# More buffers for the first 256 queries' attention, row blocks of layer 1 one step apart, one operand distance

## The chip, the cores and the metric

The kernel runs on one core of a Trainium2 chip. The metric is the device time of one execution in microseconds (us). The engines are TensorE (PE, matrix products; PEld is its loading of the stationary operand), VectorE (DVE), ScalarE (ACT), GpSimd (POOL) and SyncE (SP, which issues the DMAs here). SBUF is the on-chip memory, PSUM holds the results of products.

## The reference

Block-causal attention, 4 batches of 8 heads with 576 positions of 64, then two expert layers on the 2304 tokens. The weights are float64.

```
scores = q @ k^T / sqrt(64), masked where block_i < block_j (blocks of 64)
attn   = softmax(scores) @ v                      # 4 x 8 x 576 x 64
x      = attn as 2304 x 512
h      = x @ w_in                                 # 512 -> 2048
g      = max(h, 0) + log1p(exp(-|h|))             # softplus
x2     = g @ w_out                                # 2048 -> 512
h2     = x2 @ u_in                                # 512 -> 1024
solu   = h2 * softmax(h2)
out    = (layer_norm(solu) * g_ln) @ u_out        # 1024 -> 512
```

## The kernel before

**Number format.** Products run in fp32r. Each float32 matrix is split into a high and a low part, and a product is the sum of three (high·high, high·low, low·high). The float64 weights come as two 32-bit words and are unpacked by a `Piece` (L255): `load` (L267) on SP into one of 3 `raw` buffers, `abs` on ACT (L274), three bit steps on DVE (L277, L280, L284), the high part by a copy on ACT or DVE, and the low part by a subtraction on DVE (L294). There are 32 pieces for layer 1, 16 w1 and 16 w2.

**Attention of the first 256 queries.** `UnitA` (from L479), 16 units, unit n for batch n // 4 and a pair of heads. A unit loads qkA (256 KB) and vA (128 KB) on SP, makes scores on PE (`mm_qk`, into a PSUM bank R, r, acc or hp), masks them with a memset and takes maxima on DVE (L538, L543, L546), exponentiates on ACT into eA (L552), normalizes on DVE (four `norm` instructions, L564), transposes on PE (L571), copies the result to SBUF (`psA`), multiplies by v (`pv`), and splits the result into xt (`x_hi`, `x_lo`, L590), the input of layer 1. Buffers: qkA 3, vA 2, the small mA and dA 2 each, eA 2, psA 1. The remaining 320 queries of a batch (`UnitC`) come after all 16 units and all weights, in other banks.

**Layer 1** is made of pairs (`Pair`): pair (c, p) takes columns of row block c (256 tokens) and two of the 16 slices of the 2048 features. Block a (24 products `hp<-xt,w`, 12 for each slice) gives h; softplus follows (ACT abs, exp, ln; DVE t at L656; gh; DVE gl at L664); block b (24 products with gh, gl and w2) adds into the accumulator of the row block: acc for c = 0, R for c = 1. SEQ is the order of the pairs: for row blocks 0 and 1 it runs LAG steps ahead in row block 0; LAG is 2, so (0,0), (0,1), (1,0), (0,2), (1,1) and so on. Row blocks 2 to 8 run one after the other. **Layer 2** (`Tok`) runs on 18 tiles of 128 tokens.

**The order of everything** is computed by `Plan` (L43): a list scheduler that gives each step to its engine's queue by rank and by modelled durations. The tables OFF and RANK shift the ranks of a kind of step or of a group; MARGIN adds to the modelled latencies. The order on each engine is fixed when the program is built; the engines wait for one another by semaphores.

**Placement.** A product of 256 columns reads a stationary and a moving tile from SBUF. By the addresses of the built program, the start of the moving operand minus that of the stationary one, modulo 512 bytes, is 192 for 1512 of these 3456 products (1296 with xt and w1, 216 with gh or gl and the last w2 tiles) and 448 for the other 1944. Small tiles set it: `pad_x`, `pad_l` and the 64 extra elements in `wide`.

Of the kernel before, what the change touches and what calls it, by code (L numbers as in the profile page):

```python
# [10 lines left out]
F32 = mybir.dt.float32  # L11
F32R = mybir.dt.float32r
# [6 lines left out]


OFF = {
    "Pair.a": -160.87, "Pair.b": -32.19, "Pair.do_gh": -103.91, "Piece.bits0": 139.36, "Piece.do_lo@P": -201.40,
    "Piece.do_lo_g": 267.76, "Tok.a": 141.06, "Tok.x_hi": -460.68, "UnitA.x_hi": 408.37, "Tok.tr": -394.45,
    "Tok.bm": 359.77, "UnitC.pv": 348.22, "UnitC.tr": -288.31, "Pair.stt": -191.35, "Pair.do_gl": -445.21,
    "UnitC.qk_lo": -290.12,
}
RANK = {
# [3 lines left out]
    "Tok": (4285.47, -27.327),  # L31
}
MARGIN = {
    "PE": 600.0, "ACT": 100.0, "DVE": 100.0, "POOL": 100.0,
# [2 lines left out]
B, H, S, D = 4, 8, 576, 64  # L37
# [15 lines left out]
class Plan:  # L53
# [8 lines left out]
    def add(self, eng, dur, rank, fn, deps=(), lat=None):  # L62
        t = _Task()
        t.key = key_of(fn)

        t.alts = dict(eng) if isinstance(eng, dict) else {eng: dur}
        name, i = t.group = self.group
        t.local = rank
        t.rank = rank + RANK[name][0] + RANK[name][1] * i + OFF.get(t.key, 0.0) + OFF.get(t.key + "@" + name, 0.0)
        t.eng, t.fn, t.n, t.done = None if len(t.alts) > 1 else eng, fn, len(self.tasks), False  # L70
        t.lat = (self.LAT + (120.0 if eng == "PE" else 0.0)) if lat is None else lat
        t.users, t.left, t.ready = [], 0, 0.0
        for d in deps:
            if d is not None:
                d.users.append(t)
                t.left += 1
        self.tasks.append(t)
        return t
# [5 lines left out]
    def chain(self, eng, rank, steps, deps):  # L84
        for dur, fn in steps:
            t = self.add(dur if isinstance(dur, dict) else eng, dur, rank, fn, deps)
            deps = [t]
        return t
# [83 lines left out]
def key_of(fn):  # L172
    while isinstance(fn, partial):
        fn = fn.func
    return ".".join(fn.__qualname__.split(".")[-2:])
# [6 lines left out]
def dve_ns(n, per=1.04):  # L182
    return 70.0 + per * n
# [6 lines left out]
def dma_ns(nbytes, n=1):  # L190
    return max(50.0 + nbytes / 360.0, 550.0 * n)
# [3 lines left out]
def body(ctx: ExitStack, tc: tile.TileContext, qk, qkA, vP, vA, w1, w2, u1, u2, gln, out):  # L195
    nc = tc.nc
    PE, ACT, DVE, POOL, SP = nc.tensor, nc.scalar, nc.vector, nc.gpsimd, nc.sync
    plan = Plan()
    XTB, LAG = 3, 2
    add, chain = plan.add, plan.chain  # L200
    DMA_LAT = 1700.0

    def mm(out, lhsT, rhs, start, stop):
        PE.matmul(out, lhsT, rhs, start=start, stop=stop, skip_group_check=True)  # L204
# [9 lines left out]
    def at_of(lst, i):  # L214
        return lst[i] if 0 <= i < len(lst) else None
# [4 lines left out]
    def pool(name, side, **kw):  # L220
        return tc.tile_pool(name=name, bufs=1, side=side, reuse_waits="tile", **kw)
# [3 lines left out]
    pw = left.enter_context(pool("w", "left"))  # L225
    pl1 = left.enter_context(pool("l1", "left"))
# [4 lines left out]
    state = {}  # L231
# [3 lines left out]
    w2t = [pw.tile([128, 2, 512], F32R, name=f"w2_{f}") for f in range(12)]  # L235


    wide = [pw.tile([128, 2048 + 64 * (1 - i)], F32R, name=f"w2w_{i}") for i in range(2)]
    w2t += [t[:, 1024 * i:1024 * i + 1024].rearrange("p (h f) -> p h f", h=2) for t in wide for i in range(2)]
    lln, lhn = wide[0][:, 64:], wide[1]  # L240
    ident = pw.tile([128, 128], F32, name="ident")
    gcol = pw.tile([128, 48], F32, name="gcol")[:, 0:8]
    acc = qsh.tile([128, 2, 512], F32, name="acc")
# [76 lines left out]
    def xfree(c):  # L320

        return [t for u in pairs if u.c == c - XTB for t in (u.t_a0, u.t_a1)]
# [3 lines left out]
    class UnitC:  # L326
# [64 lines left out]
        def load_v(self):  # L391
            self.v = self.t([128, 2, 5, D], "v")
            SP.dma_start(out=self.v, in_=vP[self.b, :, 2 * self.pr:2 * self.pr + 2])
# [85 lines left out]
    class UnitA:  # L479
# [6 lines left out]
        def plan(self, prev, rank, opened):  # L486
            n = self.n = len(prev)
            p1, p2 = at_of(prev, n - 1), at_of(prev, n - 2)

            def g(u, *names):  # L490
                return [getattr(u, x) for x in names] if u else []


            self.bank = ("R", "r", "acc", "hp")[n] if n < 4 else "r" if n in (8, 9, 10, 11) else ("r", "R")[n % 2]
            free = [u.t_xl for u in prev if u.bank == self.bank][-1:]
            if n >= 12 and self.bank == "R":
                free += evacs[1]
            self.t_qk = add("SP", dma_ns(262144), rank - 2, self.load_qk, [opened] + g(p1, "t_v") + g(at_of(prev, n - 3), "t_mqk"), DMA_LAT)
            self.t_v = add("SP", dma_ns(131072), rank - 2, self.load_v, [opened, self.t_qk] + g(p2, "t_pv"), DMA_LAT)
            self.t_mqk = add("PE", 760, rank, self.mm_qk, [self.t_qk] + free)  # L500
            t = chain("DVE", rank, ((200, self.mask), (330, partial(self.max, 0)), (600, partial(self.max, 1)), (70, self.scale)), [self.t_mqk])
            t = add("ACT", 1580, rank, self.exp, [t] + g(p2, "t_tr"))
            t = chain("DVE", rank, ((72, self.den0), (90, self.den1), (918, self.norm)), [t])
            self.t_tr = add("PE", 650, rank, self.tr, [t])
            self.t_cp = add({"ACT": 708, "DVE": 870}, None, rank, self.copy, [self.t_tr] + g(p1, "t_pv"))
            self.t_pv = add("PE", 718, rank, self.pv, [self.t_cp, self.t_v])
            self.t_xh = add({"ACT": 264, "DVE": 335}, None, rank, self.x_hi, [self.t_pv] + xfree(self.b))
            self.t_xl = add("DVE", dve_ns(NA), rank, self.x_lo, [self.t_xh])
            xparts.setdefault(self.b, []).append(self.t_xl)
            prev.append(self)  # L510
# [4 lines left out]
            SP.dma_start(out=self.qk, in_=qkA[self.b, self.pr])  # L515

        def load_v(self):
            self.v = self.t([128, 2, 2, D], "vA")
            SP.dma_start(out=self.v, in_=vA[self.b, self.pr])

        def mm_qk(self):

            if self.bank == "hp":
                self.st = [x.rearrange("p a b -> p (a b)")[:, None, :] for x in hps]
            else:
                self.st = [{"R": state["R"], "r": state["r"], "acc": acc}[self.bank]]

            self.banks = [x[:, j] for x in self.st for j in range(x.shape[1])]
            self.m, self.den = self.t([128, 2, 2], "mA"), self.t([128, 2, 2], "dA")
            for i, sl in enumerate(QA):  # L530
                for j in range(2):
                    h = slice(64 * j, 64 * j + 64)
                    mm(self.banks[j][:, sl], self.qk[h, 128 * i:128 * i + 128], self.qk[h, 256:384 + 128 * i], i == 0, i == 1)
# [12 lines left out]
            DVE.tensor_scalar(self.m, self.m, 0.125, None, op0=ALU.mult)  # L546

        def exp(self):
            self.e = state["eA"][self.n % 2]
            for i, sl in enumerate(QA):  # L550
                for j in range(2):
                    ACT.activation(self.e[:, j, sl], self.banks[j][:, sl], AF.Exp, scale=0.125,  # L552
                                   bias=self.m[:, i, j:j + 1], accum_out=self.den[:, i, j:j + 1])
# [17 lines left out]
                    PE.transpose(self.banks[j][:, sl], self.e[:, j, sl], ident)  # L571

        def copy(self, e):
            self.ps = self.t([128, 2, 384], "psA", 1)
            w = 2 // len(self.st)
            for j, st in enumerate(self.st):
                copy(e, self.ps[:, w * j:w * j + w], st[:, :, 0:384])
# [111 lines left out]
    def open_a():  # L689
        state["pat"] = right[0].enter_context(pool("atA", "right"))  # L690
        state["pcv"] = right[0].enter_context(pool("cvA", "right"))
        q = right[0].enter_context(pool("qaA", "right", space=PSUM))
        state["R"] = q.tile([128, 2, 512], F32, name="R")
        state["r"] = q.tile([128, 2, 512], F32, name="r")
        state["eA"] = [state["pat"].tile([128, 2, 384], F32, name=f"eA{n}") for n in range(2)]
        make_identity(nc, ident)

    def conv_a(what, n):
# [37 lines left out]
    def open_q():  # L736
        psl.close()
        state["qtr"] = left.enter_context(pool("qtr", "left", space=PSUM))
        pl1.tile([128, 24], F32, name="pad_l")

    NR, NCA = 3, 4
    t_open = add("POOL", 500, 0.0, open_a, ())
# [20 lines left out]
    for kind, f in todo:  # L763
        src, t, done = (w1[f], w1t[f], w1ready) if kind == "w1" else (w2[f * 128:f * 128 + 128, :], w2t[f], w2ready)
# [30 lines left out]
    for f in range(8):  # L795
        p = Piece(u2[f * 128:f * 128 + 128, :], w_of(w1t[6 + f], 0), w_of(w1t[6 + f], 1), gcol[:, f:f + 1])
        n = len(upieces) % 3
# [226 lines left out]
```

## Time and profile before

| | |
|---|---|
| median of 3 runs | 810.62 us (808.69 to 810.79) |
| the profiled execution | 811.79 us |
| its span in the trace | 810.02 us |
| mean granted TensorE clock | 0.989 of 2.4 GHz |
| PE busy | 783.8 us (97% of the span), 5752 products |
| DVE busy | 568.3 us (70%) |
| ACT busy | 394.0 us (49%) |

Times in the trace count from the start of the span. The first acc product (block b of pair (0,0)) starts at 46.88, the last R product ends near 152.48, and layer 2 takes over between 498.81 and 634.89. PE has 97% of the span, so a row says something about the time where PE is idle or its clock is low.

### The profile page before, as it was taken

How to read it: one execution, taken by the hardware profiler on the slowest of the kernel's cores; microseconds unless marked ns; L12 is line 12 of the kernel's file. 1: busy time of each engine (PE TensorE's matmuls, PEld its weight loads, DVE VectorE, ACT ScalarE, POOL GpSimd, SP SyncE). 2: the span in 40 equal slices, each digit the busy share in tenths (PEclk: the TensorE clock that was granted, in tenths of full speed). 3: DMA queues.
4: the chain of work that ended last, by engine and by line, in shares of the span. 5: the costliest groups of instructions: out<-in, count | busy, mean ns of one | idle time of the engine just before them, and what ended most of it. 6: DMA issues, size and time to landing. Idle time of an engine off the chain costs nothing.

```text
span 810.0 us, 14410 instructions
## 1 busy us (share of the span) xinstructions
PE 783.8 (97%) x5752; PEld 694.7 (86%) x5752; DVE 568.3 (70%) x1291; ACT 394.0 (49%) x877; POOL 0.7 (0%) x6
## 2 busy tenths in 40 slices
PE   5689999999999999999999999999999999999998
PEld 3478989999888888888888889999898888888887
DVE  6989998565777667667776763768968486766661
ACT  5567776454565455555555553555633232322231
POOL 0000000000000000000000000000000000000000
PEclk9799999999999999999999999999999999999999
DMA  5636542202021112112112200227201111110001
GB/s 179 205 123 190 180 149 77 92 11 79 26 83 41 47 61 67 42 41 68 42 42 57 68 27 27 80 81 249 74 32 43 54 41 42 52 40 27 27 26 53
DMA packets 31203, 59.64 MB, mean 74 GB/s; under 512 B 2849, under 2 KB 14369, under 8 KB 31137
## 3 DMA queue, kind: packets, MB, share of 16 engines
q1 hardware_dynamic: 31136, 58.74, 22.9%
q8 instruction: 45, 0.74, 0.4%
q14 instruction: 22, 0.17, 0.1%
HBM read 49.29 MB, written 9.44 MB: 72 GB/s over the span
## 4 chain that ended last, share of the span: by engine, by line
PE 81%; DVE 8%; DMA 6%; ACT 3%; issue 1%; SPq 0%; ACTq 0%; DVEq 0%
PE hp L204 20%; PE acc L204 18%; PE op L204 12%; PE h L204 11%; PE S L204 5%; PE O L204 5%; PE T L452 4%; DMA raw_u<-in_u_dram 2%; DMA raw<-in_w_dram 2%; PE R L204 2%; PE tp L920 2%; PE r L204 1%; DVE a L284 1%; DVE eA L564 1%; DVE a L280 1%
## 5 line engine op out<-in xcount | busy, mean ns | idle before, releaser
L204 PE MATMUL hp<-xt,w 128*128 128x256 f32 x1728 | 221.6, 284 | 3.7 <-DVE t L656 3.4
L204 PEld LDWEIGHTS hp<-xt,w 128*128 128x128 f32 x1728 | 206.8, 189 | 9.5 <-DVE t L656 5.5
L204 PE MATMUL acc<-gh,w 128*128 128x256 f32 x768 | 148.1, 284 | 0.0
L204 PEld LDWEIGHTS acc<-gh,w 128*128 128x128 f32 x768 | 122.3, 189 | 0.7 <-issue 0.7
L204 PE MATMUL acc<-gl,w 128*128 128x256 f32 x384 | 107.3, 280 | 0.6 <-DVE gl L664 0.6
L204 PE MATMUL op<-w,w2w 128*128 128x512 f32 (+1 forms) x456 | 102.3, 382 | 0.0
L204 PE MATMUL h<-u,w 128*128 128x512 f32 x432 | 101.0, 391 | 0.0
L204 PEld LDWEIGHTS h<-u,w 128*128 128x128 f32 x432 | 80.6, 188 | 16.4
L204 PEld LDWEIGHTS op<-w,w2w 128*128 128x128 f32 x456 | 81.5, 188 | 15.3
L432 ACT ACTIVATE eC<-S,mC 128x384 f32<-128x384 f32 (+2 forms) x80 | 51.8, 649 | 46.4 <-DVE mC L421 46.4
L204 PEld LDWEIGHTS acc<-gl,w 128*128 128x128 f32 x384 | 72.5, 189 | 0.9 <-DVE gl L664 0.8
L656 DVE SCALAR_TENSOR_TENSOR t<-hp,t 128x512 f32<-128x512 f32 x72 | 49.4, 686 | 24.8 <-ACT t L653 24.2
L210 ACT ACTIVATE ps<-T 128x512 f32<-128x512 f32 (+1 forms) x74 | 40.8, 551 | 51.7 <-PE T L452 50.1
L647 ACT ACTIVATE t<-hp 128x512 f32<-128x512 f32 x72 | 42.8, 594 | 34.8 <-DVE gl L664 19.4
L664 DVE TENSOR_TENSOR gl<-t,gh 128x512 fp32r<-128x512 f32 x72 | 49.6, 690 | 3.8 <-ACT gh L210 2.4
L204 PE MATMUL acc<-gh,w2w 128*128 128x256 f32 x256 | 49.8, 285 | 0.0
L417 DVE TENSOR_REDUCE mC<-S 128x2 f32<-128x768 f32 (+2 forms) x48 | 46.9, 976 | 1.5 <-PE S L204 0.4
L650 ACT ACTIVATE t<-t 128x512 f32<-128x512 f32 x72 | 45.5, 633 | 1.8
L653 ACT ACTIVATE t<-t 128x512 f32<-128x512 f32 x72 | 45.2, 628 | 1.3
L452 PE MATMUL T<-ident,eC 128*128 128x128 f32 x288 | 45.3, 275 | 0.0
L872 ACT ACTIVATE e<-h,mx 128x1024 f32<-128x1024 f32 x18 | 20.1, 1116 | 50.5 <-PE tp L920 48.6
L926 ACT ACTIVATE w2w<-tp 128x512 fp32r<-128x512 f32 x36 | 20.7, 596 | 46.2 <-PE op L204 41.4
(156 smaller groups left out, 1128.6 us busy)
## 6 DMA issues: line engine op xcount, KB each, us to landing
raw<-in_w_dram SPq DMA_DIRECT2D x32, 512.0 KB, 4.0
qkC<-in_qk_dram SPq DMA_DIRECT2D x16, 480.0 KB, 3.4
raw_u<-in_u_dram SPq DMA_DIRECT2D x11, 512.0 KB, 3.6
v<-in_vP_dram SPq DMA_DIRECT2D x16, 320.0 KB, 2.9
x2s<-stg SPq DMA_DIRECT2D x18, 256.0 KB, 2.1
xr<-x2s SPq DMA_DIRECT2D x18, 256.0 KB, 3.2
qkA<-in_qkA_dram SPq DMA_DIRECT2D x16, 256.0 KB, 3.4
out_dram<-ob SPq DMA_DIRECT2D x15, 256.0 KB, 2.0
```

The source lines that it names most:

```text
L204: PE.matmul(out, lhsT, rhs, start=start, stop=stop, skip_group_check=True)
L210: ACT.activation(out, a, AF.Copy)
L417: DVE.tensor_reduce(out=self.m[:, 0:n], in_=self.scores(i), axis=AX.X if i < 2 else AX.XY, op=ALU.max, negate=True)
L432: ACT.activation(e, sc, AF.Exp, scale=0.125, bias=m[:, j:j + 1], accum_out=den[:, j:j + 1])
L452: PE.transpose(T[:, 128 * k:128 * k + 128], e[:, 128 * k:128 * k + 128], ident)
L647: ACT.activation(self.t, self.hp, AF.Abs)
L650: ACT.activation(self.t, self.t, AF.Exp, scale=-1.0)
L653: ACT.activation(self.t, self.t, AF.Ln, bias=1.0)
L656: DVE.scalar_tensor_tensor(out=self.t, in0=self.hp, scalar=0.0, in1=self.t, op0=ALU.max, op1=ALU.add)
L664: DVE.tensor_sub(self.gl, self.t, self.gh)
L872: ACT.activation(self.e, self.hh, AF.Exp, bias=self.mx, accum_out=self.ss)
L926: ACT.activation(self.lh[:, 4 * g:4 * g + 4, :], self.tp[g], AF.Copy)
```

## The change

The tables OFF and RANK get new values, so that the scheduler makes another order. LAG becomes 1. vA, mA, dA and eA get four buffers, psA two, and the dependencies follow: the exponential of a unit waits for the transposes of the fourth unit before it (it was the second), the copy to psA for the pv of the second before it (it was the first), the load of qkA no longer for the load of the previous vA but of the previous qkA, the load of vA also for the previous vA and the pv of the fourth before it. The scratch for DMA descriptors is set to 4096 bytes for a partition, which frees SBUF for the buffers. The pads change so that all 3456 products of 256 columns have the distance 448.

```diff
 OFF = {
-    "Pair.a": -160.87, "Pair.b": -32.19, "Pair.do_gh": -103.91, ...
+    "Pair.a": -75.59, "Pair.b": 18.34, "Pair.do_gh": 35.44, ...
...
 RANK = {
-    "first": (278.93, 20.397), "A0": (636.85, 83.080), "A1": (-4008.02, 57.487), ...
+    "first": (278.93, 20.397), "A0": (-2733.73, 86.246), "A1": (-2328.74, -30.508), ...
...
-    XTB, LAG = 3, 2
+    XTB, LAG = 3, 1
...
-    wide = [pw.tile([128, 2048 + 64 * (1 - i)], F32R, name=f"w2w_{i}") for i in range(2)]
+    wide = [pw.tile([128, 2048 + 64 * (2 - i)], F32R, name=f"w2w_{i}") for i in range(2)]
...
-    lln, lhn = wide[0][:, 64:], wide[1]
+    lln, lhn = (t[:, 64:] for t in wide)
...
-            self.t_qk = add(... [opened] + g(p1, "t_v") + g(at_of(prev, n - 3), "t_mqk"), DMA_LAT)
-            self.t_v = add("SP", dma_ns(131072), rank - 2, ... + g(p2, "t_pv"), DMA_LAT)
+            p4 = at_of(prev, n - 4)
+            self.t_qk = add(... [opened] + g(p1, "t_qk") + g(at_of(prev, n - 3), "t_mqk"), DMA_LAT)
+            self.t_v = add("SP", dma_ns(131072), rank - 1, ... + g(p1, "t_v") + g(p4, "t_pv"), DMA_LAT)
...
-            t = add("ACT", 1580, rank, self.exp, [t] + g(p2, "t_tr"))
+            t = add("ACT", 1580, rank, self.exp, [t] + g(p4, "t_tr"))
...
-            self.t_cp = add(... self.copy, [self.t_tr] + g(p1, "t_pv"))
+            self.t_cp = add(... self.copy, [self.t_tr] + g(p2, "t_pv"))
...
-            self.v = self.t([128, 2, 2, D], "vA")
+            self.v = self.t([128, 2, 2, D], "vA", 4)
...
-            self.m, self.den = self.t([128, 2, 2], "mA"), self.t([128, 2, 2], "dA")
+            self.m, self.den = self.t([128, 2, 2], "mA", 4), self.t([128, 2, 2], "dA", 4)
...
-            self.e = state["eA"][self.n % 2]
+            self.e = state["eA"][self.n % 4]
...
-            self.ps = self.t([128, 2, 384], "psA", 1)
+            self.ps = self.t([128, 2, 384], "psA", 2)
...
-        pl1.tile([128, 24], F32, name="pad_l")
+        pl1.tile([128, 88], F32, name="pad_l")
...
-    nc = _bacc.Bacc("TRN2", target_bir_lowering=False, num_devices=1)
+    nc = _bacc.Bacc("TRN2", target_bir_lowering=False, num_devices=1, dynamic_dma_scratch_size=4096)
```

What it does to the order shows best on PE just ahead of the first acc product. Before, in the rows from the first product block on (hp_114 and hp_115 are the two hp banks, w_0_81 and w_0_97 the first slices of w1 and w2):

```order
L204 MATMUL hp_114<-xt,w_0_81 128x256 x12
L571 MATMUL R<-ident,eA_131 128x128 x6
L204 MATMUL hp_114<-xt,w_1_82 128x256 x12
L204 MATMUL r<-qkA 128x128 x2
L204 MATMUL r<-qkA 128x256 x2
L204 MATMUL R<-psA,vA 64x256 x2
L204 MATMUL R<-psA,vA 64x128 x2
L204 MATMUL hp_115<-xt,w_2_83 128x256 x12
L204 MATMUL hp_115<-xt,w_3_84 128x256 x12
L204 MATMUL R<-qkA 128x128 x2
L204 MATMUL R<-qkA 128x256 x2
L204 MATMUL acc<-gh,w_0_97 128x256
```

The same place of PE after the change:

```order
L205 MATMUL R<-qkA 128x128 x2
L205 MATMUL R<-qkA 128x256 x2
L205 MATMUL r<-qkA 128x128 x2
L205 MATMUL r<-qkA 128x256 x2
L205 MATMUL hp_114<-xt,w_1_82 128x256 x12
L573 MATMUL R<-ident,eA_133 128x128 x6
L573 MATMUL r<-ident,eA_132 128x128 x6
L205 MATMUL R<-psA,vA 64x256 x2
L205 MATMUL R<-psA,vA 64x128 x2
L205 MATMUL r<-psA,vA 64x256 x2
L205 MATMUL r<-psA,vA 64x128 x2
L205 MATMUL acc<-gh,w_0_97 128x256
```

The a block of pair (0,1) (w_2_83, w_3_84) no longer stands ahead of the first acc product; two units (the 7th and 8th) are scored, transposed and multiplied by v there instead.

Behind block b of pair (0,0), PE had the a blocks of pairs (1,0) and (0,2) with b(0,1) ahead of them:

```order
L204 MATMUL acc<-gh,w_3_100 128x256
L204 MATMUL hp_114<-xt,w_0_81 128x256 x12
L204 MATMUL hp_114<-xt,w_1_82 128x256 x12
L204 MATMUL hp_115<-xt,w_4_85 128x256 x12
L204 MATMUL hp_115<-xt,w_5_86 128x256 x12
L571 MATMUL r<-ident,eA_130 128x128 x6
L204 MATMUL hp_114<-xt,w_2_83 128x256 x12
```

After the change, right behind b(0,0), whose last product has w_1_98:

```order
L205 MATMUL acc<-gh,w_1_98 128x256
L205 MATMUL hp_115<-xt,w_0_81 128x256 x12
L205 MATMUL hp_115<-xt,w_1_82 128x256 x12
L205 MATMUL hp_114<-xt,w_2_83 128x256 x12
L205 MATMUL hp_114<-xt,w_3_84 128x256 x12
L205 MATMUL r<-qkA 128x128 x2
L205 MATMUL r<-qkA 128x256 x2
L205 MATMUL hp_115<-xt,w_2_83 128x256 x12
```

Pair (1,0) now follows (0,0) directly, and (0,1) and (1,1) follow with their a blocks before the first b block into R.

On SP, the loads from the third unit's qkA on, before (raw is a weight piece):

```order
L515 DMA qkA<-in_qkA_dram 128x512
L269 DMA raw<-in_w_dram 128x1024 x3
L519 DMA vA<-in_vA_dram 128x256
L515 DMA qkA<-in_qkA_dram 128x512
L269 DMA raw<-in_w_dram 128x1024
```

And after:

```order
L517 DMA qkA<-in_qkA_dram 128x512
L521 DMA vA<-in_vA_dram 128x256
L270 DMA raw<-in_w_dram 128x1024
L517 DMA qkA<-in_qkA_dram 128x512
L521 DMA vA<-in_vA_dram 128x256
L517 DMA qkA<-in_qkA_dram 128x512 x2
L270 DMA raw<-in_w_dram 128x1024
```

The units' loads moved ahead of the second and third weight piece.

## Rows read from the trace of the kernel before

**Rows 1.** Windows of PE: stretch, length, busy (products), granted clock, DMA share, GB/s.

```profile
3.54:46.88 43.34, 30.50 (x196) 0.84 0.56 188
46.88:152.48 105.60, 100.68 (x846) 0.98 0.44 139
152.48:498.81 346.33, 346.33 (x2891) 1.00 0.16 50
498.81:634.89 136.08, 134.39 (x989) 1.00 0.28 90
```

**Rows 2.** Windows at half clock: busy of PE, PEld, DVE, ACT, POOL, then clock.

```profile
25.49:32.32 6.83, 4.96 (x22) 3.19 (x22) 6.78 (x25) 4.68 (x16) 0.00 (x0) 0.50 0.30 92
35.73:39.15 3.42, 3.42 (x19) 2.90 (x16) 3.39 (x11) 1.66 (x3) 0.00 (x0) 0.50 0.95 307
52.80:56.21 3.41, 3.32 (x17) 2.61 (x18) 2.71 (x9) 2.06 (x5) 0.00 (x0) 0.50 0.22 55
```

**Rows 3.** Waits of PE (total, times, longest): 46.88 to 152.48; the last, 498.81 to 634.89.

```profile
PE r L204 <- ACT psA L210: 2.1, 1, 2.1
PE hp L204 <- DVE t L656: 2.0, 2, 1.5
PE acc L204 <- DVE gl L664: 0.6, 1, 0.6
...
PE hp L204 <- DVE t L656: 1.4, 2, 1.0
```

**Rows 4.** Timeline of PE, 20 to 52: start, duration, instruction, [idle before <-releaser].

```profile
27.07 1.65 PE L204 MATMUL R<-qkA 64*128 64x128 f32 x8 [4.16 <-DMA qkA<-in_qkA_dram]
28.65 1.54 PE L571 MATMUL hp<-ident,eA 128*128 128x128 f32 x6
...
32.34 0.88 PE L571 MATMUL r<-ident,eA 128*128 128x128 f32 x6
35.44 1.31 PE L204 MATMUL r<-psA,vA 128*64 128x256 f32 x8 [2.23 <-DVE psA L212]
36.68 2.79 PE L204 MATMUL hp<-xt,w 128*128 128x256 f32 x12
...
39.88 1.62 PE L204 MATMUL hp<-xt,w 128*128 128x256 f32 x12
41.42 0.93 PE L204 MATMUL r<-qkA 64*128 64x128 f32 x8
42.28 0.87 PE L204 MATMUL R<-psA,vA 128*64 128x256 f32 x8
...
46.88 0.39 PE L204 MATMUL acc<-gh,w 128*128 128x256 f32 x1
```

**Rows 5.** Timeline of DVE: third unit's maximum, small steps, norms, weight shift, gl, last weight.

```profile
9.61 1.02 DVE L543 TENSOR_REDUCE mA<-acc 128x2 f32<-128x256 f32 x2 [0.48 <-ACT eA L552]
10.55 0.16 DVE L556 TENSOR_SCALAR dA<-dA 128x4 f32<-128x4 f32 x1
...
10.96 1.01 DVE L564 TENSOR_SCALAR eA<-eA,dA 128x128 f32<-128x128 f32 x4
...
13.21 0.76 DVE L277 TENSOR_SCALAR a<-a 128x512 int32<-128x512 int32 x2
...
45.52 0.67 DVE L664 TENSOR_TENSOR gl<-t,gh 128x512 fp32r<-128x512 f32 x1
...
136.72 0.69 DVE L294 TENSOR_TENSOR w2w<-a,w2w 128x512 fp32r<-128x512 f32 x1
```

**Rows 6.** Pieces of the chain of waits: start, duration, what (number of products).

```profile
130.67 5.44 PE hp L204 x48
...
180.74 2.74 PE acc L204 x24
...
187.30 2.83 PE acc L204 x24
...
507.29 5.71 PE hp L204 x48
```

More of the change, by code (lines that the diff above doesn't have):

```diff
@@ L21 @@
 OFF = {
[L22 to L25, printed above, removed]
+    "Pair.a": -75.59, "Pair.b": 18.34, "Pair.do_gh": 35.44, "Piece.bits0": 156.91, "Piece.do_lo@P": -117.94,
+    "Piece.do_lo_g": 39.95, "Tok.a": 311.98, "Tok.x_hi": -596.65, "UnitA.x_hi": 667.22, "Tok.tr": -141.11,
+    "Tok.bm": 453.62, "UnitC.pv": 162.36, "UnitC.tr": -166.97, "Pair.stt": -175.92, "Pair.do_gl": -199.23,
+    "UnitC.qk_lo": -536.59, "Piece.do_hi": -94.45, "UnitA.copy": 176.03, "UnitA.exp": 182.87,
+    "UnitA.norm": 173.41, "Piece.abs": 751.71, "Piece.load": -87.26,
 }
 RANK = {
[3 rows of a table removed]
-    "Tok": (4285.47, -27.327),
[3 rows of a table added]
+    "Tok": (4184.20, -7.771),
 }
@@ L497, in plan @@
                 free += evacs[1]
-            self.t_qk = add("SP", dma_ns(262144), rank - 2, self.load_qk, [opened] + g(p1, "t_v") + g(at_of(prev, n - 3), "t_mqk"), DMA_LAT)
-            self.t_v = add("SP", dma_ns(131072), rank - 2, self.load_v, [opened, self.t_qk] + g(p2, "t_pv"), DMA_LAT)
+            p4 = at_of(prev, n - 4)
+            self.t_qk = add("SP", dma_ns(262144), rank - 2, self.load_qk, [opened] + g(p1, "t_qk") + g(at_of(prev, n - 3), "t_mqk"), DMA_LAT)
+            self.t_v = add("SP", dma_ns(131072), rank - 1, self.load_v, [opened, self.t_qk] + g(p1, "t_v") + g(p4, "t_pv"), DMA_LAT)
             self.t_mqk = add("PE", 760, rank, self.mm_qk, [self.t_qk] + free)
             t = chain("DVE", rank, ((200, self.mask), (330, partial(self.max, 0)), (600, partial(self.max, 1)), (70, self.scale)), [self.t_mqk])
-            t = add("ACT", 1580, rank, self.exp, [t] + g(p2, "t_tr"))
+            t = add("ACT", 1580, rank, self.exp, [t] + g(p4, "t_tr"))
             t = chain("DVE", rank, ((72, self.den0), (90, self.den1), (918, self.norm)), [t])
             self.t_tr = add("PE", 650, rank, self.tr, [t])
-            self.t_cp = add({"ACT": 708, "DVE": 870}, None, rank, self.copy, [self.t_tr] + g(p1, "t_pv"))
+            self.t_cp = add({"ACT": 708, "DVE": 870}, None, rank, self.copy, [self.t_tr] + g(p2, "t_pv"))
             self.t_pv = add("PE", 718, rank, self.pv, [self.t_cp, self.t_v])
@@ L694, in open_a @@
         state["r"] = q.tile([128, 2, 512], F32, name="r")
-        state["eA"] = [state["pat"].tile([128, 2, 384], F32, name=f"eA{n}") for n in range(2)]
+        state["eA"] = [state["pat"].tile([128, 2, 384], F32, name=f"eA{n}") for n in range(4)]
         make_identity(nc, ident)
```

6 rows, old and new, of the table RANK are left out of this document.

## The prediction

> **What bounds the kernel now.** TensorE (PE) is busy in 97% of the span, by the table above. The windows of PE say where its idle time is [rows 1]: 43.34 − 30.50 = 12.84 us before 46.88 (the first acc product), 105.60 − 100.68 = 4.92 us between there and 152.48 (the last R product of layer 1's second row block), none in the next 346 us, 136.08 − 134.39 = 1.69 us up to 634.89. From 152 on the time is the products themselves: an edit helps only if it takes idle time out of the first 152 us or the late 1.69 us, or makes products shorter. The granted clock is the second reading: from 52.80 to 56.21 it is 0.50, the 1.2 GHz level, with PE busy in 3.32 of 3.41 us [rows 2]; half of that work is lost, 1.66 us. The stretch from 46.88 to 152.48 so loses 4.92 + 1.66 = 6.6 us in all, its waits being for the one psA buffer's copy (2.1), t (2.0) and gl (0.6) [rows 3].
>
> What holds PE up ahead of 46.88 is VectorE (DVE): in the stretch 25.49 to 32.32 DVE is busy for 6.78 of 6.83 us while PE is busy for 4.96 [rows 2]. So the first acc product comes when DVE has worked off what stands ahead of its gl. PE's own waits there, for loads of qkA too (4.16 us at 27.07) [rows 4], hardly count: the work that the load released was not what DVE was short of.
>
> **The change, part by part.** The profiled run took 811.79 us (span 810.02 and 1.8 around it), 1.17 above the median 810.62; I work out a difference against the first and apply it to the second.
>
> *First acc product.* The new order finishes units 6 and 7 ahead of block b of pair (0,0), and block a of pair (0,1) behind it. DVE's instructions from the third unit's maximum (9.61) to the first gl are counted in both orders. The new one has 8 more norms, 2 more maxima, one more memset, 5 more of the four-element kind, one weight shift and one xt cast less; all else is equal. By their rows [rows 5]: two groups of four norms 2 × 1.01, two maxima 1.02, the small ones and the memset 6 × 0.16 = 0.96, less 0.76/2 = 0.38 for the shift and half of that, 0.2, for the cast, which is half as wide: 3.4 us. An instruction starts before the row ahead of it ends (9.61 + 1.02 = 10.63, and the next at 10.55); at 0.05 for each of the 14 that are more, 2.7 us are left. One wait goes: the third unit's maximum waited 0.48 for the exponential that held an mA buffer, and there are four of them now [rows 5]. The gl that ended at 45.52 + 0.67 = 46.19 then ends at 48.4, and with 0.5 for the gap (46.88 − 46.19 = 0.69 before, with a unit's scores in between [rows 4]) the product starts at 48.9: **+2.0**. Both ends: with no DVE wait anywhere and less in the gap 46.6, and with 2 us of new DVE waits for exponentials 51. I take the middle because DVE has the weight pieces to fill in. The third vA load now goes ahead of all weight loads on SP, and two of the first three weight loads behind later units' loads; who waits for that is DVE, which has a unit's work instead, so I put it at nothing; if that cover fails it is inside the 51.
>
> *From there to the last R product.* Counted on PE: two a blocks more (5.44/4 = 1.36 each, by the chain's 48 products in 5.44) [rows 6], one unit's transposes (0.88) and two units' pv (0.87 each) less [rows 4]: 2.72 − 0.88 − 1.74 = **+0.1**. Behind it, one set of transposes less is still to do: **−0.8** with its gap.
>
> *Waits in that stretch.* The 2.1 for psA goes with its second buffer. The waits for t and gl go where PE has other work. With rows one step apart PE has b(0,0), a(1,0), a(0,1), a(1,1), b(1,0) ready in a row, about 14 us, in which DVE gets ahead. Against that stands the clock: PE does little in the ten microseconds ahead of 48.9, and I expect a stretch at the 1.2 GHz level just behind it, 3.4 us long as two of the three shown are, 1.7 lost [rows 2]. With 0.8 for small waits 2.5 of the 6.6 stay: **−4.1**. The ends: all of it stays (0), or all goes (−6.6). DVE's last weight piece ended at 136.72 + 0.69 = 137.4, about 15 us ahead of the last product that needs it [rows 5]; in the new order it comes about 1 us later, so this slack holds.
>
> *Late.* Two waits for t cost 1.4 us at the turn to layer 2 [rows 3]. The first token tile's block now stands one pair further behind its last maximum, and the pairs alternate regularly; I take half, **−0.7** (bounds −1.7, and +1.5 for one more wait as long as the longest for t [rows 3]).
>
> *Distance.* All 3456 products of 256 columns get 448 bytes between the starts of their two operands (modulo 512); before, 1512 had 192. The chain shows two rhythms: 48 products in 5.44 us (113 ns each) or 5.71 (119 ns). At 192 both occur (hp at 130.67 and at 507.29), and at 448 too (acc 24 in 2.74 at 180.74, in 2.83 at 187.30) [rows 6]. The rhythm is set anew behind each interruption and kept through the block. So the sum takes 0. Bounds: if the distance leans the choice by 2.3 ns for 1512 products −3.5; if all were 119 ns, some +9. The Trainium skill, page "SBUF — State Buffer", section "Who interferes with whom", gives PE two independent read ports, one for the moving operand and one for the weight load; by it no distance could matter, and this part would be worth exactly 0. The rhythms in the trace don't follow the distance, which agrees, though nothing here shows the ports. The smaller DMA scratch only makes room: every DMA of this kernel is issued on SP.
>
> Sum: +2.0 + 0.1 − 0.8 − 4.1 − 0.7 = **−3.5**: 811.79 becomes 808.3 and the median 810.62 becomes **807.1**.
>
> **The rivals.**
> *A. The waits come back.* The second buffer and the step of one only move the wait from PE's psA to t and gl: with a step of one, a block of row 1 follows its partner of row 0 at once, and the softplus between a and b (three ScalarE passes, then t, gh and gl) has fewer products to hide under. For it: t and gl already make 2.6 of the 4.7 us of waits [rows 3]. Against it: DVE's slack of 15 us. If 6.6 stays lost and the late 1.7 too: +2.0 + 0.1 − 0.8 = +1.3, 811.9.
> *B. The clock: slower.* PE's work between 28 and 49 us is thinner now (two a blocks less), between waits on DVE. If the 1.2 GHz level holds through it, the rows tell the price [rows 4]: two half a blocks 2 × (2.79 − 1.62) = 2.3, four sets of transposes 4 × (1.54 − 0.88) = 2.6, four pv 4 × (1.31 − 0.87) = 1.8, two scores 2 × (1.65 − 0.93) = 1.4: 8.1 us if all of it is on the path to the first acc. Then −3.5 + 8.1 = +4.6, less up to 0.8 for small waits that the longer front lets DVE clear: 814.4 to 815.2. It breaks even when the first acc product comes at 48.9 + 3.5 = 52.4 and is slower by 0.3% from 54.8 on. For it: the clock was at 0.50 in stretches of the old front, from 25.49 and from 35.73 [rows 2]. Against it: DVE bounds the front, so longer products there mostly fill gaps. [...]
> *C. One distance does pay.* If 192 is what brings on the slower rhythm part of the time, the 3.5 of the bound comes on top: 803.6. For it: the first products behind transposes fall into the slow rhythm somewhat more often at 192. Against it: both rhythms at both distances [rows 6].
> The change not doing what it says is no case: the built order has the units, pairs and distances as described.
>
> **How the numbers follow.** Forecast 0.50, with its own range of 804.5 to 809.7 from the clock and DVE-wait terms; A 0.20 (810 to 813); B 0.17; C 0.13. A measurement of this kernel can tell about 0.3%, here 808.19 and 813.05. Faster: three quarters of the forecast's range lies below 808.19, with C 0.51. Slower: B's 0.17 and the edge of A, 0.19. Within 0.3%: the rest, 0.30. The range leaves out B and half of C's lower edge: 802 to 813.
>
> **What would show it.** First acc product at 48 to 50 us; 52.4 or later speaks for B, with granted clock 0.50 through 35 to 49. PE's idle time from there to the last R product at 1 to 2 us with no wait on psA, one stretch at 0.50 right at its start; 4 to 5 us of waits for t and gl speak for A. Last R product at 150 to 151, about 2 earlier than 152.48 for the end of the last product. Idle time around the turn to layer 2 under 1.2 us. Between, the same 346 us of products, the rhythm of hp and acc blocks mixed as before; if it takes 343 or less, C is right. The prediction is wrong if the stretch without waits gets longer or shorter by over 1 us, which no term here but the distance can do.

## The result

The changed kernel takes 801.12 us (median of 4 runs, 800.63 to 802.22); the ratio to the kernel before is 0.9888 (95% interval 0.9869 to 0.9906). That is some 9.1 us by the ratio and 8.5 by the medians. The forecast was −3.5 us. The direction was right, the size was not: 801.12 lies below the range of 802 to 813.

These are the windows of PE in the profiled execution (802.22 us, span 800.4) that answer to [rows 1]. Their bounds are the first acc product, the last R product, the last attention product and the first product with layer 2's second matrix; the columns are stretch, length, busy (products), granted clock, DMA share, GB/s:

```profile
0.00:47.73 47.73, 31.63 (x201) 0.83 0.61 199
47.73:147.34 99.61, 98.83 (x848) 1.00 0.44 143
147.34:490.75 343.41, 343.41 (x2872) 1.00 0.16 49
490.75:625.29 134.54, 133.82 (x1000) 1.00 0.28 91
```

The first acc product is 0.85 us later (47.73 against 46.88). The stretch behind it is 99.61 us instead of 105.60, with 0.78 us of idle time instead of 4.92 and a clock of 1.00. PE's waits in it, answering to [rows 3], show that the psA wait and those for t are gone:

```profile
PE r L205 <- DVE xt L592: 0.5, 1, 0.5
PE acc L205 <- DVE gl L666: 0.2, 1, 0.2
```

By the forecast's steps, in us of the profiled runs (811.79 and 802.22):

| step | forecast | measured |
|---|---|---|
| start to first acc product | +2.0 | +0.85 |
| first acc to last R product | −4.0 | −5.99 |
| behind the last R product (654.03 to 649.57 from its start to that of the very last product) | −1.5 | −4.46 |
| sum | −3.5 | −9.6 |

The half clock did not go away; it moved. In the changed kernel PE is at 0.50 in these two windows ahead of the first acc product (and, like the kernel before, in a short one near 12 us). Behind that product only 0.95 us are left at 0.50, where the kernel before had 3.41 [rows 2]:

```profile
25.00:31.00 6.00, 4.80 (x22) 0.50 0.27 94
42.00:48.00 6.00, 5.09 (x26) 0.50 0.56 174
47.73:48.68 0.95, 0.95 (x6) 0.50 0.63 141
```

VectorE's instructions at the front's two ends are these (timeline: start, duration, instruction):

```profile
8.82 1.02 DVE L545 TENSOR_REDUCE mA<-acc 128x2 f32<-128x256 f32 x2
...
46.31 0.68 DVE L666 TENSOR_TENSOR gl<-t,gh 128x512 fp32r<-128x512 f32 x1
```

The third unit's maximum starts 0.79 us earlier than in [rows 5] and gl ends at 46.99, 0.80 later, not 2.2.

### The profile page after: what moved, and what is told of

It is laid out like the page before. It is cut to its first block, busy times and chain, and to the rows that moved or that the text cites. A ratio compares the mean times of both kernels' runs of the same rounds, so it can differ in the third digit from the quotient of the medians.

```text
span 800.4 us, 14451 instructions
## 1 busy us (share of the span) xinstructions
PE 779.6 (97%) x5752; PEld 692.3 (86%) x5752; DVE 561.1 (70%) x1299; ACT 406.2 (51%) x869; POOL 0.7 (0%) x6
## 4 chain that ended last, share of the span: by engine, by line
PE 75%; DVE 14%; DMA 5%; ACT 3%; issue 2%; SPq 0%; ACTq 0%; DVEq 0%
PE hp L205 16%; PE acc L205 16%; PE op L205 12%; PE h L205 12%; PE S L205 5%; PE O L205 5%; PE T L453 4%; DMA raw_u<-in_u_dram 3%; PE tp L922 2%; PE R L205 2%; DVE t L658 2%; DVE a L281 1%; DVE a L285 1%; DVE gl L666 1%; DVE mA L545 1%
## 5 line engine op out<-in xcount | busy, mean ns | idle before, releaser
L205 PE MATMUL hp<-xt,w 128*128 128x256 f32 x1728 | 218.2, 281 | 0.0
L211 ACT ACTIVATE ps<-T 128x512 f32<-128x512 f32 (+1 forms) x55 | 30.7, 559 | 23.4 <-PE T L453 23.3
```

The lines of the kernel that those rows point to most:

```text
L211: ACT.activation(out, a, AF.Copy)
```

## The experiments

Medians and ratios to the kernel before, measured beside each. First acc, last R and PE's idle time between them are from one profile each.

| run | median us | ratio (95%) | first acc | last R | idle |
|---|---|---|---|---|---|
| before | 809.65 | 1 | 46.88 | 152.48 | 4.92 |
| after | 801.12 | 0.9888 (0.9869–0.9906) | 47.73 | 147.34 | 0.78 |
| e1 after, old pads | 801.89 | 0.9896 (0.9874–0.9918) | 48.97 | 147.68 | 0.02 |
| e2 before, new pads | 810.94 | 1.0011 (0.9996–1.0027) | 46.84 | 152.41 | 4.50 |
| e3 after, distance 192 | 801.62 | 0.9900 (0.9874–0.9925) | 48.61 | 146.89 | 0.37 |
| e4 after, step of two | 813.15 | 1.0037 (1.0020–1.0054) | 50.17 | 156.56 | 5.62 |
| e5 after, old buffers | 819.61 | 1.0102 (1.0076–1.0128) | 53.71 | 163.76 | 3.82 |
| e6 before, step of one | 816.00 | 1.0058 (1.0036–1.0079) | 45.81 | 156.10 | 7.12 |
| e7 before, step of one, new buffers | 809.86 | 0.9991 (0.9979–1.0002) | 41.59 | 153.70 | 5.19 |
| e8 after, two norms on ACT | 803.52 | 0.9909 (0.9893–0.9926) | 48.66 | 150.29 | 1.04 |
| e9 after, one bit step less | 799.81 | 0.9857 (0.9838–0.9877) | 48.38 | 146.83 | 0.00 |
| e10 after, no 1e-9 | 801.59 | 0.9880 (0.9861–0.9899) | 48.15 | 148.03 | 1.00 |
| e11 as e10, scaling on GpSimd | 806.67 | 0.9945 (0.9929–0.9960) | 47.83 | 153.17 | 4.37 |
| e12 after, one psA | 813.99 | 1.0037 (1.0021–1.0052) | 39.51 | 152.91 | 8.19 |
| e13 after's order, one psA | 808.21 | 0.9964 (0.9950–0.9979) | 52.71 | 152.91 | 0.95 |
| e14 after's order, two eA, mA, dA | 803.23 | 0.9910 (0.9887–0.9934) | 49.38 | 149.42 | 0.86 |
| e15 before's order, new buffers | 809.82 | 0.9990 (0.9974–1.0007) | 44.95 | 148.69 | 4.47 |
| e16 after, PE kept busy in two gaps | 802.33 | 0.9898 (0.9876–0.9919) | 48.65 | 147.51 | 0.70 |
| e17 after, all gaps filled | 800.80 | 0.9874 (0.9835–0.9912) | 46.16 | 145.58 | 0.66 |
| e18 after, last gap filled | 801.18 | 0.9884 (0.9837–0.9931) | 47.75 | 147.34 | 1.08 |

**The distance: e1, e2, e3.** e1 has the pads of before in the changed kernel, e2 the new pads (and the smaller scratch) in the kernel before, and e3 64 elements more behind the weights of the changed kernel.

```diff
e1
-    wide = [pw.tile([128, 2048 + 64 * (2 - i)], ...
+    wide = [pw.tile([128, 2048 + 64 * (1 - i)], ...
...
-        pl1.tile([128, 88], F32, name="pad_l")
+        pl1.tile([128, 24], F32, name="pad_l")
e3
-    gcol = pw.tile([128, 48], ...
+    gcol = pw.tile([128, 112], ...
```

> The changed kernel with the pads of before: 1512 of the 3456 products of 256 columns are back at the distance 192, the order of all instructions stays. Theory W (the whole gain is idle time and clock that PE no longer loses; the distance is worth nothing): the time of the changed kernel, 800 to 802 us, and the same PE idle time. Theory D (about 3 us of the gain are products that run faster at one distance): 803.5 to 805 us, the 346 us stretch from the last R product to the last O product longer by 1 to 2 us at unchanged idle time.

> The kernel before with the new pads (and the smaller scratch, which makes the room for them): all 3456 products at 448, the order of before. W: no difference, 809 to 811 us, ratio within 0.2% of 1. D: 806 to 807.5 us, and the stretch without waits (346.2 us in before) at 344 to 345.

> The changed kernel with 64 more elements behind the weights: 3024 of the 3456 products at the distance 192 instead of 448, the same order. W: 800 to 802 us. D with 2.3 ns a product: 3024 x 2.3 ns = 7 us more, 808 us; any excess over e1 should be twice that of e1.

All three went as W said. These are the windows of the stretch without waits in e1, e3 and e2, in this order, to be read beside 343.41 of after and 346.33 of [rows 1]:

```profile
147.68:490.96 343.28, 343.28 (x2872) 1.00 0.16 49
...
146.89:490.30 343.41, 343.41 (x2872) 1.00 0.16 49
...
152.41:498.74 346.33, 346.33 (x2891) 1.00 0.16 50
```

The stretch is 343.3 or 343.4 us in the new order and 346.3 in the old, whichever the distance. So rival C falls. The two orders' windows don't hold the same products: by a count in the traces the new one has 12 acc products and one unit's six transposes fewer. They come to about 2.0 of the 2.9 us, and the acc products only stand behind the window now. That the stretch keeps its length at either distance bears out what the forecast drew from the Trainium skill's "SBUF — State Buffer", "Who interferes with whom", that the distance cannot matter, with 0.1 us of difference over some 2900 products (two distances were tried), though no run here shows the ports themselves.

**One part undone or done alone, the scheduler free: e4 to e7, e12.**

```diff
e4
-    XTB, LAG = 3, 1
+    XTB, LAG = 3, 2
e6
-    XTB, LAG = 3, 2
+    XTB, LAG = 3, 1
e12
-            self.ps = self.t([128, 2, 384], "psA", 2)
+            self.ps = self.t([128, 2, 384], "psA", 1)
-            ... self.copy, [self.t_tr] + g(p2, "t_pv"))
+            ... self.copy, [self.t_tr] + g(p1, "t_pv"))
```

e5 is the changed kernel with all buffer lines and dependencies of before, e7 the kernel before with those of after and the step of one.

> The changed kernel with row blocks 0 and 1 two steps apart again, its buffers, tables and pads kept; the scheduler makes the order anew. If the step of one removes the waits for t and gl (2.6 us in before): 803 to 805 us, with such waits back between the first acc and the last R product. If the buffers alone remove them: 800 to 802 us.

> The changed kernel with the buffers and dependencies of before (vA, mA, dA, eA two, psA one), its tables, pads and the step of one kept. Theory L (the step of one is what empties the stretch of waits; the buffers bring the psA wait of 2.1 and the half clock behind it, 1.7): 803 to 805 us, with waits on psA back. Theory B (the buffers bring most of it): 807 to 810 us.

> The kernel before with the step of one alone; old tables, buffers and pads. L: the stretch from the first acc to the last R product, 105.6 us before, loses 3 to 5 us, 805 to 807 us, the wait for psA (2.1) remaining. B: 809 to 811 us, with the same waits as before.

> The kernel before with the step of one and the new buffers, the old tables and pads. If step and buffers are the whole of it and the tables only fit the order to them: 801 to 803 us. If the new tables (units 7 and 8 ahead of the first acc) are needed: 804 to 808 us, with PE idle time of 3 us or more between first acc and last R.

> The changed kernel with one psA buffer (and the copy waiting for the previous unit's pv), all other buffers kept; the scheduler makes the order anew. If the buffer is worth the wait that it removes and the half clock behind it: 2.1 + 1.7 us more, 803 to 806 us. If the other buffers (eA, mA, dA, vA) carry the gain: 801 to 802.5 us.

None of the theories had these sizes. Each edit gives the scheduler another order, and every such order is at 809.9 us or more; e5, e6, e4 and e12 are slower than the kernel before. In each the idle time between first acc and last R is 3.8 to 8.2 us. e12 shows that an early first acc product is worth nothing by itself: it comes at 39.51, 8 us sooner than in the changed kernel, and the last R product 5.6 us later. These runs don't show that a step of two or old buffers must be slow; they show that the tables fit one combination. The new tables alone, with the old step and buffers, were not tried.

**Buffers apart from the order: e13, e14, e15.** Here the order on every engine is that of after (e13, e14) or before (e15), and the numbers of buffers alone are changed. By the traces PE, VectorE and ScalarE run the same instructions in the same order in e13 and e14 as in after. In e14 some units' exponentials are overwritten before they are transposed, so that its output is not the reference's: it does the same work, but does not say what two such buffers would cost a kernel that keeps the data.

```diff
e13
-            self.ps = self.t([128, 2, 384], "psA", 2)
+            self.ps = self.t([128, 2, 384], "psA", 1)
e14
-            self.e = state["eA"][self.n % 4]
+            self.e = state["eA"][self.n % 2]
-            ... self.t([128, 2, 2], "mA", 4), self.t([128, 2, 2], "dA", 4)
+            ... self.t([128, 2, 2], "mA"), self.t([128, 2, 2], "dA")
```

> The order of the changed kernel on every engine kept word for word, with one psA buffer instead of two. (In the run with one psA buffer before, the scheduler also made another order.) If the buffer itself is worth what that run lost: 811 to 815 us. If the order carries the gain, the buffer costs only the waits that this order then has: the copies of every second unit of a pair wait for a pv, 0.5 to 1.5 us for each of a few pairs on the path: 802 to 806 us.

> The order of the changed kernel kept, with two eA, mA and dA buffers instead of four (psA two, vA four). If the order carries the gain: the maxima of the third and fourth unit wait for exponentials and these for transposes, some 0.5 to 2 us ahead of the first acc product: 802 to 804 us. If the buffers carry it: 808 us or more.

> The order of the kernel before kept on every engine, with the new numbers of buffers (vA, mA, dA, eA four, psA two; smaller scratch for the room). If the buffers remove the wait for psA by themselves: the 2.1 us at 52.9 and the half clock behind it go, 806 to 808 us. If that wait comes from the order (the copy stands late on ScalarE) or DVE takes the time back: 809 to 811 us.

e13 lost 6 to 7 of the 9 us, more than the few waits that were expected. Its stretch from first acc to last R is 100.20 us with 0.95 idle, as in after; 5.0 of the 6.3 us between the two profiled executions lie ahead of the first acc product, at 52.71. These are the timeline and windows of PE in e13:

```profile
44.83 1.70 PE L573 MATMUL R<-ident,eA 128*128 128x128 f32 x6 [4.04 <-DVE eA L566]
47.09 1.69 PE L573 MATMUL r<-ident,eA 128*128 128x128 f32 x6 [0.56 <-DVE eA L566]
48.71 1.55 PE L205 MATMUL R<-psA,vA 128*64 128x256 f32 x8
51.23 1.55 PE L205 MATMUL r<-psA,vA 128*64 128x256 f32 x8 [0.97 <-ACT psA L211]
52.71 0.58 PE L205 MATMUL acc<-gh,w 128*128 128x256 f32 x1
...
25.00:37.00 12.00, 8.71 (x39) 0.50 0.45 141
45.00:54.00 9.00, 7.47 (x34) 0.50 0.47 169
```

The copies that wait for the one buffer stand between two pv of half-clock length (1.55 instead of 0.87), and the clock is at 0.50 for over 12 and over 9 us, where after has it for under 7 each time. This is what rival B described: a first acc product behind 52.4 would have taken the whole gain that was forecast; of the larger one that there is some 3 us are left. How the loss divides between the copies' waits and the clock was not separated. The second psA buffer keeps both away. Two vA buffers in this order were not tried. e14's first acc product is 1.65 us later than after's and its median 2 us higher, with intervals that overlap.

e15 says the other half: the new buffers in the old order give nothing (0.9990, interval 0.9974 to 1.0007). Its waits between first acc and last R are those of [rows 3]:

```profile
PE r L204 <- ACT psA L210: 2.1, 1, 2.1
PE hp L204 <- DVE t L656: 1.5, 1, 1.5
PE acc L204 <- DVE gl L664: 0.6, 1, 0.6
```

The wait of 2.1 for the psA copy is there with two buffers. PE's transposes that the copy reads and ScalarE's instructions ahead of it in e15, and the pv that waits:

```profile
47.87 1.13 PE L571 MATMUL r<-ident,eA 128*128 128x128 f32 x6
...
49.77 0.48 ACT L552 ACTIVATE eA<-R,mA 128x256 f32<-128x256 f32 x1
50.13 0.21 ACT L552 ACTIVATION_READ_ACCUMULATOR eA<-R,mA 128x1 f32 x1
50.22 0.82 ACT L210 ACTIVATE psA<-r 128x768 f32<-128x768 f32 x1
...
51.09 0.87 PE L204 MATMUL r<-psA,vA 128*64 128x256 f32 x8 [2.09 <-ACT psA L210]
```

The transposes end at 49.00, and the copy starts at 50.22, right behind another unit's exponentials on ScalarE. It stood late in ScalarE's order; the second buffer was there and did not help. In e13, with the new order and one buffer, PE has no such wait behind the first acc product. So it was the order that removed this wait, and not the buffer, as the forecast had put it.

**What holds the front: e8 to e11.** e8 moves two units' norms to ScalarE, and the scheduler makes another order for it. e9 leaves out one bit step of each weight piece, so that its weights lose their signs and its output is not the reference's. e10 leaves out the 1e-9, and e11 moves the scaling to GpSimd as well; e9 to e11 keep the order.

```diff
e8
...
-   DVE.tensor_scalar(self.e[:, j, sl], ..., self.den[:, i, j:j + 1], None, op0=ALU.mult)
+   ACT.activation(self.e[:, j, sl], ..., AF.Copy, scale=...)      # units 4 and 6
e9
-            DVE.scalar_tensor_tensor(out=self.a, in0=self.raw[:, :, 1], scalar=-0x80000000, ...
e10
-            DVE.tensor_scalar_add(self.den, self.den, 1e-9)
e11
-            DVE.tensor_scalar(self.m, self.m, 0.125, None, op0=ALU.mult)
+            POOL.tensor_scalar(self.m, self.m, 0.125, None, op0=ALU.mult)
```

> The changed kernel with the normalization of the fifth and seventh unit (four instructions each) on ScalarE instead of VectorE. VectorE has no idle time from 8.5 to 48 us in the changed kernel, so if it alone sets the first acc product, that comes 1.5 to 1.9 us sooner (two groups of norms of 0.92) and the time is 799 to 800 us. If the longer instructions on ScalarE (four of 0.4 instead of 0.25) delay what VectorE waits for: first acc at 47.7 or later, 801 us or more.

> The changed kernel without the second bit step of each weight piece (the sign bit is left out of the unpacked weights), one VectorE instruction of 0.60 us less in each of the 32 pieces of layer 1, 19 us of VectorE work. In all kernels so far the last weight piece ends at 136 to 138 us whatever the order. Theory V (VectorE's own work sets the first 137 us, PE fills in what it can): the last piece ends at 118 to 121, first acc 2 to 4 us sooner, last R product 5 to 8 us sooner, 792 to 796 us. If loads or ScalarE take over as the bound at once: last piece at 128 or later and 798 us or more.

> The changed kernel without the addition of 1e-9 to a unit's sums of exponentials (that addition is left out; the sums are at least 1, where it changes nothing in float32), one small VectorE instruction for each of the 16 units, about 0.12 us each from start to start; the order is otherwise the same. V: 8 of them before the first acc product, 16 in all, so the time falls by 0.5 to 1.9 us against the changed kernel's 801.1 to 801.9: 799.5 to 801. If a saving on VectorE there is not passed on: 801 to 802.

> As the run before (1e-9 left out), and the scaling of a unit's maxima by 0.125 on GpSimd, which is idle, instead of VectorE: another small instruction (0.15 us) less for each unit on VectorE, and two semaphores and GpSimd's latency more between maximum and exponential. V: another 0.5 to 1.5 us less than the run before. If the longer chain from maximum to exponential makes VectorE wait for the exponentials: the same time or 1 to 3 us more, with idle time of VectorE in 8.5 to 48 us that the changed kernel doesn't have.

My theory V, that VectorE's own work sets the first 137 us, fell with e9: with 19 us less of it the median falls by 1.3 us (0.9857 against 0.9888, intervals that overlap), the first acc product doesn't come sooner, and the last weight piece ends at 135.24 instead of 137.26. Between 8.50 and the first acc product VectorE is idle for 3.55 of 39.88 us in e9, against 0.44 of 39.23 in after. The windows from first acc to the last weight piece, of e9 and of after (busy of PE, PEld, DVE, ACT, POOL) are:

```profile
48.38:135.24 86.86, 86.86 (x747) 83.24 (x746) 74.00 (x166) 59.48 (x122) 0.00 (x0) 0.99 0.48 153
...
47.73:137.26 89.53, 88.77 (x761) 84.87 (x760) 86.17 (x190) 59.72 (x122) 0.00 (x0) 0.99 0.46 149
```

PE is busy all the time there, in after but for 0.76 us, and VectorE merely follows. Behind its first acc product the changed kernel is PE's. e10's saving is too small to see. e8's first acc product is 0.9 us later and the stretch behind it 2 us longer (101.63); as its order differs, it doesn't say what ScalarE's work alone costs. e11's first acc product comes at 47.83, as in after, so the longer path from maximum to exponential costs the front nothing that shows. Its lost time lies behind that product, where VectorE waits for ScalarE and PE for VectorE:

```profile
DVE t L658 <- ACT t L655: 5.3, 4, 2.4
DVE dA L561 <- ACT eA L554: 2.3, 2, 1.9
...
PE r L573 <- DVE eA L566: 2.2, 2, 1.4
PE r L205 <- DVE xt L592: 1.6, 2, 1.0
```

**The clock ahead of the first acc product: e16, e17, e18.** These runs put products of no use into acc, which is free then, in PE's idle stretches.

```diff
e16, behind block a of pair (0,0) (34 in e17, e18)
+                for _ in range(28):
+                    mm(acc[:, 0, 0:CT], w[:, 0, 0, :], x[:, 0, 0, :], True, True)
e16, behind the fourth unit's pv (20 in e17)
+                for _ in range(14):
+                    mm(acc[:, 0, 0:128], ident, ident, True, True)
e17, e18: 4 more behind the eighth unit's transposes; e17: 3 behind the sixth's
```

> The changed kernel with work without use on PE in its two longest idle stretches ahead of the first acc product: 14 products of the 128x128 identity with itself behind the fourth unit's pv (idle from 21 to 25.9 us) and 28 products of 256 columns behind block a of pair (0,0) (idle from 36.8 to 41.1), into acc, which is free then. If the granted clock stays at its upper level through them, the transposes and pv behind them take half (1.70 to 0.9, 1.5 to 0.9), the chain to the first acc product is 2 to 4 us shorter and the time 797 to 800 us. If the other engines set the chain anyway: 801 to 802 us. If the work without use stands in the way: 802 us or more.

> As run 16, with the idle stretches ahead of the first acc product filled almost whole: 20 identity products behind the fourth unit's pv, 3 behind the transposes of the sixth unit, 34 products of 256 columns behind block a of pair (0,0), 4 identity products behind the transposes of the eighth unit. In run 16 the granted clock still fell to 0.5 from 26.8 to 34.7 and from 43.9 to 48.9, behind gaps of 0.8 to 1.5 us that were left. If these gaps bring it down: no stretch at 0.5 between 21 and 49 us, the transposes, pv and a block there 3 to 5 us shorter, first acc at 45 to 47 and 797 to 800 us. If VectorE sets the chain even so (its maxima from 36 to 45 us are on it): first acc at 47 to 48.5 and 800 to 802 us. If the clock falls all the same: 801 to 804 us.

> Only the later part of run 17: 34 products of 256 columns behind block a of pair (0,0) and 4 identity products behind the eighth unit's transposes. If it keeps the clock up from 41 to 48: the transposes of the seventh unit and the two pv take 2 us less, first acc at 45.5 to 46.5, 799 to 800 us. If the clock falls all the same: 801 to 803 us.

In e16 the clock fell behind both fillings all the same, at 27.7 and 44.8 us (a closer reading than the one in the next run's expectation). In e17 it stays at 1.00 where after has 0.50. Its windows, and the timeline of PE at the end of the front, followed by the same two products in after and in e18:

```profile
25.00:31.00 6.00, 4.90 (x39) 1.00 0.31 96
42.00:48.00 6.00, 5.12 (x41) 1.00 0.49 170
...
45.36 0.87 PE L205 MATMUL r<-psA,vA 128*64 128x256 f32 x8
46.16 0.39 PE L205 MATMUL acc<-gh,w 128*128 128x256 f32 x1
47.03 0.39 PE L205 MATMUL acc<-gl,w 128*128 128x256 f32 x1 [0.48 <-DVE gl L674]
...
47.73 0.58 PE L205 MATMUL acc<-gh,w 128*128 128x256 f32 x1
48.10 0.42 PE L205 MATMUL acc<-gl,w 128*128 128x256 f32 x1
...
47.75 0.38 PE L205 MATMUL acc<-gh,w 128*128 128x256 f32 x1
48.43 0.39 PE L205 MATMUL acc<-gl,w 128*128 128x256 f32 x1 [0.29 <-DVE gl L671]
```

The pv take 0.87 again, the first acc product is ready 1.6 us sooner, and then the second one waits for gl, which VectorE ends at 46.98 (46.37 + 0.61 by the chain), the same as after's 46.99. So in the changed kernel PE at half clock ends the front some 1.1 us after VectorE would let it (48.10 against 47.03), and 0.9874 against 0.9888 is no difference that these intervals tell. e18 has the pv at 0.87 too, but its whole front ran 0.8 us later from the fourth unit's pv on (21.03 against 20.26), its second product waits for gl as in e17, and its median is that of after. No kernel here beats the changed one by more than the intervals while computing all of it.

## Why the forecast was too small

The step that failed most is the forecast's term for the products' spacing. It took 0 there, because it held that only the distance between the operands could change the rhythm. The runs show at two distances that the distance does nothing, and that the products behind the last R product, with the pauses between them, take some 2.5 to 3 us less in the new order. Two terms for waits were mis-sized besides: a VectorE wait of 1.21 us was left out, and of the 2.5 us that were kept for PE's waits and half clock about 1.3 came. The parts follow.

*First acc product: +2.0 forecast, +0.85 measured.* The count of VectorE's instructions was right; what failed here is the waits. I took off 0.48 us. VectorE had another wait in the old front, which I left out:

```profile
42.48 0.27 DVE L538 MEMSET r<- 64x256 f32 x1 [1.21 <-PE r L204]
```

It is gone in the new order, and the third unit's maximum starts 0.79 sooner. The count of 2.7 less 1.21 is 1.5, less 0.79 is 0.7; measured 0.80. That VectorE bounds the front, and not PE's clock, did not hold in the changed kernel: PE at half clock came last, by 1.1 us (e17).

*First acc to last R: −4.0 forecast, −5.99 measured.* The mechanism held: waits for psA, t and gl go, PE has work in hand. The size was off by the 2.5 us that I kept. 1.7 of it was a stretch at half clock put behind the first acc product. It lies ahead of it instead, and only its last 0.95 us reach behind, 0.5 lost (PE's first acc product takes 0.58 at 47.73 against 0.39 [rows 4]). The rest, 0.8, was measured as 0.78. The +0.1 for the work in the stretch came as about −0.7; why stays open. One reason was wrong: the psA wait goes with the order, not with the second buffer (e15); what the buffer does in the new order is to keep the front short (e13).

*Behind the last R: −1.5 forecast, −4.46 measured.* One unit's transposes less and the waits for t at the turn to layer 2 were named. The transposes account for −0.6. The waits gave −0.97 by the idle time of the windows (1.69 to 0.72) instead of −0.7, since both for t went and only 0.6 us of others came. The rest of about −2.9 is in the products' spacing, which the forecast put at nothing. By the starts of all products there, the mean spacing of 256-column products within blocks falls from 115.7 to 115.2 ns over some 2470 products, 1.3 us; pauses of about 0.2 us between two of them are 114 instead of 121, 0.8 us; the changes between blocks and other work give the other 0.8. One profile's noise is part of these figures: from the last R product to the very last, the ten profiles of the new order (after, e1, e3, e9, e10, e13, e14, e16 to e18) take 648.0 to 650.7 us, and the three of the old one (before, e2, e15) 652.8 to 654.0, 4.2 us more in the mean. I had read that both rhythms occur at both distances, and that was right, but it left the order as what chooses between them, and a new order was the change. What in an order favours the quicker rhythm stays open: e1 and e3, at other distances, have 115.1 and 115.2, and e2, at the new one, 116.0.

The forecast's own sign of being wrong came, too: the stretch without waits got 2.9 us shorter, "which no term here but the distance can do". It was not the distance. Some 1.4 us of it are products that stand behind the stretch now, 0.6 the transposes, and the rest, some 0.9, the spacing for the most part.

*The rivals.* A did not happen: t is not waited for between first acc and last R. B happened in e13 and not in the changed kernel. The time even fell below C's 803.6, for another reason than C's.

*What I had not seen.* The parts are not to be summed one by one. The forecast gave each edit a price of its own; the runs say that buffers without the order are worth nothing (e15), the order and the other buffers with one psA buffer some 3 us (e13), the step alone less than nothing (e6), all together 9.

## What to carry to other kernels

Where a scheduler's tables, buffers and a loop's step were changed together, undo one with the order kept and one with the order free: the two say different things. A buffer's wait is the buffer's only if the instruction that fills it stood ready; otherwise it is the order's. Where a time is forecast by adding up one engine's work, that engine's own waits belong into the sum, each one that the change removes. A stretch without waits can change its length as well, by which products stand in it and by their spacing.

## What the runs showed of the hardware

Products of one shape, 128x256 in fp32r, start at one of two spacings, about 113.4 or 118 ns, mostly kept through a block behind its first two or three products. Moving the start of one operand against the other from 448 to 192, modulo 512 bytes, for 1512 or 3024 products left the stretch at 343.3 to 343.4 us (e1, e3), and the opposite move left it at 346.33 (e2).

The granted clock fell to the 1.2 GHz level behind small gaps too: in e16 PE was busy from 21.48 to 24.87 and from 38.17 to 41.63, then idle for 1.46 and 0.75 us, busy for a unit's transposes, and idle for another 0.86 and 1.13 us. These windows of PE show the clock behind that:

```profile
26.50:27.70 1.20, 0.89 (x6) 1.00 0.07 27
27.80:34.50 6.70, 6.18 (x30) 0.50 0.51 148
43.50:44.70 1.20, 0.07 (x2) 1.00 0.79 290
44.90:48.20 3.30, 3.24 (x18) 0.50 0.45 150
```

With the gaps filled as well (e17) it stayed up through these stretches. The same order of work can meet different clocks: e15's profiled execution, 807.14 us and the shortest of its ten, was at 1.00 from 52 to 57 us, where the kernel before has 0.66 in its own:

```profile
52.00:57.00 5.00, 4.97 (x41) 1.00 0.46 175
...
52.00:57.00 5.00, 4.11 (x23) 0.66 0.31 82
```

This may be part of the spread of the kernel before from 807 to 814 us. Its 21 executions measured beside e15 fit that: the three with a mean granted clock of 0.997 or 0.998 took 807.2 to 808.6 us, the five at 0.985 or 0.987 took 809.9 to 812.6. It is not the whole, as executions at 0.989 lie between 808.6 and 814.3 in the round of e17.
